# Another written order of the opening's steps and first loads in a fused attention and mixture kernel

## The chip, the cores and the metric

One core of one Trainium2 chip. The metric is the device time of one execution in microseconds. Five instruction streams matter: PE (TensorE, matmuls), DVE (VectorE), ACT (ScalarE), POOL (GpSimd) and SP (SyncE, which issues the input transfers).

## The reference, cut to what matters

```python
# q, k, v: 8 batches x 8 heads x 576 positions x 64, float32
scores = q @ k.T / 8
mask: heads 0-3 the last 32 positions, heads 4-7 every 32nd position before
attn = softmax(where(mask, scores, -1e9))        # max, exp, sum, divide
x = (attn @ v), heads side by side               # 4608 tokens x 512
h = maximum(maximum(x @ w1, x @ w2), x @ w3)     # 512 -> 768
out = h @ w_out                                  # 768 -> 512
```

## The kernel before, in words

The products `x @ w` are made in two parts: a float32 value is split into a high part (`xh`, `hh`) and a low part (`xl`, `hl`) that TensorE multiplies exactly enough, and the weights are split alike. Most of the program's later part (lines 789 and 887) works on sums of weights that the opening builds and writes to a scratch area in memory. The opening computes the first attention units, the first 512 tokens of the mixture directly (lines 522 and 552), and prepares the weights.

The order of the opening is written out by hand as a string of steps, `OPENING`; a loop executes it, and `pin` keeps each engine's instructions in that written order. A step is a letter and a number. One attention unit `n` (one batch, a pair of heads; units 0 to 3 belong to batch 0, 4 to 7 to batch 1, unit 8 to batch 2) passes through:

- `S n` scores on PE: for batch 0 first a mask matmul (L306), then L337, or L315 for the strided units from 4 on; `U n` (ACT L292) first copies the unit's keys into pairs for L315
- `X n` the masking and the maximum on DVE (L358, L366 and L367; for units in `APART` L358, L363 and L364)
- `E n` exponentials on ACT (L383, one instruction), or `G n` exponentials apart (L375, ten instructions with their sums, ten more records); units 2 and 7 are apart in both versions
- `N n` probabilities and the transpose on DVE (L394 to L397, L404)
- `V n` the product with v on PE (L481, L441 or L470), `H n` its high part (ACT L495), `L n` its low part (DVE L500)

A weight tile passes through `A` (ACT L164, POOL L165), `K` (ACT L170), `B` (DVE L180 and L183), `D` (POOL L193) and `C` (ACT cast L202, POOL L203). `F n` is 12 matmuls of line 522 into one result tile (two result tiles, used in turn), and `f`/`g` are the two halves of one of these: `f` needs units 1 and 0's columns (features 256 to 511), `g` those of units 2 and 3. `M n` reads the result out. `O n` is 18 matmuls of line 552, `Q n` its store, `T` prepares the second chunk of tokens, `W n` issues the writes of built weights to scratch from SP.

Scores have two places in TensorE's result memory. One serves units 0 and 2, the other, `s_ps` of pool `ps_s`, all the others, so `S8` may start only when the transpose of unit 7 (L404 in `N7`) has read it:

```python
s_ps = s_places[0 if n in (0, 2) else 1]
```

`LOADS` is the order in which SP issues the first input transfers: `q n` is the queries' piece and then the keys' piece of unit n, `v n` pieces of v, `w n` one weight tile each. SP is one queue, and a transfer whose buffer or semaphore isn't free holds up those behind it. From unit 4 on, `S n` also issues the q load of unit n+2.

Of the kernel before, what the change touches and what calls it, by code (L numbers as in the profile page):

```python
# [50 lines left out]
A12, A11, A22, S4, S2, S1, S3 = range(7)  # L51
# [1 line left out]


LOADS = """
q0 q0 w0 w1 q1 w2 q1 w3 v0 w4 w5 q2 q2 v0 v0 v0 w6 q3 q3 v1 v1 v1 v2 v2 v2 v1 v4 v2 w7 w8 v2 w9 v5 q4 q4 v3 v3 v3 v3
v3 w10 w11 v4 v4 w12 w13 q5 v4 v5 v5 v5 q5
"""
OPENING = """
S0 A0 X0 K0 A1 K1 K2 B0 D0 S1 B1 E0 N0 D1 A2 C0 S2 A3 B2 C1 A4 X1 B3 B4 K3 X2 D2 K4 E1 D3 N1 C2 C3 A5 A6 K5 V0 H0 L0  # L60
B5 B6 S3 D4 X3 D5 K6 D6 G2 C4 N2 C5 C6 E3 V1 H1 L1 V2 A7 A8 W0 N3 K7 A9 H2 f0 f1 U4 K8 K9 B7 S4 B8 D7 D8 C7 L2 V3 C8
H3 L3 A10 A11 W2 g0 B9 D9 M0 K10 K11 g1 F2 B10 D10 M1 C9 K12 X4 A12 C10 A13 F3 M2 F4 B11 K13 M3 F5 B12 E4 N4 U5 M4 D11
D12 C11 A14 C12 S5 M5 F6 F7 B13 B14 D13 K14 K15 K16 V4 K17 W3 X5 M6 M7 D14 F8 C13 A15 A16 C14 A17 B15 W1 D15 B16 D16
M8 E5 B17 N5 D17 K18 F9 M9 F10 A18 F11 C15 B18 M10 C16 K19 C17 A19 A20 K20 M11 S6 K21 X6 F12 B19 A21 D18 E6 W7 B20 D19
D20 W5 M12 F13 H4 F14 C18 K22 M13 F15 C19 C20 W4 A22 A23 K23 N6 B21 D21 V5 S7 M14 H5 B22 M15 B23 F16 F17 D22 D23 X7
C21 C22 C23 M16 M17 V6 T2 W8 O0 O1 G7 N7 H6 U8 T3 Q1 Q0 V7 S8 X8 O2 T0 Y0 Z0 U9 H7 E8 Q2 N8 Y1 O3 T1 Q3 W6
"""
APART = [int(step[1:]) for step in OPENING.split() if step[0] == "G"]

# [920 lines left out]
```

## Time and profile before

| | us |
|---|---|
| median of 3 runs | 668.78 (666.77 to 670.19) |
| the profiled execution | 667.13 |
| its span in the profile | 665.4 |
| PE busy in the span | 643.8 (97%) |
| DVE, ACT, POOL busy | 370.4, 337.3, 301.5 |

The profiled execution's time holds 1.7 us around its span. Numbers in square brackets in a row of the timeline are the idle time of the engine just before, with what ended it. Busy shares are means over stages with different limits: PE is busy without a break from 43.8 us on, and has its gaps ahead of that.

### The profile page before, as it was taken

What the parts mean: (1) busy time and instruction counts of PE and PEld (TensorE: products, weight loads), DVE (VectorE), ACT (ScalarE), POOL (GpSimd) and SP (SyncE); (2) the same over time, 40 slices, a digit from 0 to 9 for tenths busy, and PEclk for the clock granted to TensorE, in tenths of its full rate; (3) what the DMA queues carried; (4) which work ended last, traced back from release to release, by engine and by line L of the source; (5) the groups of instructions that cost most, each with busy time, mean ns of one, the idle gap of its engine ahead of it and who ended that gap; (6) DMA issues with size and microseconds to landing.
All of it is one profiled execution on the core that took longest, in us unless ns stands there. A gap on an engine that the chain in (4) does not pass through costs nothing.

```text
span 665.4 us, 18035 instructions
## 1 busy us (share of the span) xinstructions
PE 643.8 (97%) x7408; PEld 553.0 (83%) x7408; DVE 370.4 (56%) x515; ACT 337.3 (51%) x702; POOL 301.5 (45%) x291
## 2 busy tenths in 40 slices
PE   4599999999999999999999999999999999999997
PEld 3478888788778988988888888889999888999986
DVE  5878866576774647378355665743264662314340
ACT  4867666344364445546455456544444564444441
POOL 8979998799932423420233424004432402444410
PEclk9989999999999999999999999999999999999999
DMA  9799956747689777752487787336966614777411
GB/s 303 228 262 376 331 162 215 233 156 245 186 270 346 254 235 238 246 189 79 151 300 237 246 257 234 119 107 172 285 211 190 177 64 131 218 217 215 122 47 64
DMA packets 89370, 138.36 MB, mean 208 GB/s; under 512 B 10152, under 2 KB 39592, under 8 KB 89288
## 3 DMA queue, kind: packets, MB, share of 16 engines
q1 hardware_dynamic: 85256, 129.86, 62.1%
q10 hardware_dynamic: 4032, 7.34, 3.0%
q8 instruction: 59, 0.97, 0.6%
q14 instruction: 23, 0.19, 0.1%
HBM read 111.21 MB, written 25.95 MB: 206 GB/s over the span
## 4 chain that ended last, share of the span: by engine, by line
PE 81%; POOL 8%; DMA 1%; SPq 1%; ACT 1%; issue 1%; DVE 1%; POOLq 0%; DVEq 0%; ACTq 0%
PE f_ps L789 46%; PE f_ps L887 17%; PE f_ps L522 9%; PE f_ps L552 3%; POOL work L593 2%; PE o_ps L441 2%; PE o_ps L470 2%; PE s_ps L315 2%; POOL work L585 2%; POOL work L609 1%; PE s_ps L337 1%; POOL hl L543 1%; POOL sums_low L593 1%; POOL sums_low L585 1%; POOL sums_low L609 1%
## 5 line engine op out<-in xcount | busy, mean ns | idle before, releaser
L789 PE MATMUL f_ps<-xc,w_stream 128*128 128x448 f32 x1512 | 315.6, 368 | 0.6 <-DMA w_stream<-scratch 0.3
L789 PEld LDWEIGHTS f_ps<-xc,w_stream 128*128 128x128 f32 x1512 | 281.6, 188 | 27.4 <-ACT snap L840 2.3
L840 ACT COPY snap<-f_ps 128x448 f32<-128x448 f32 x240 | 128.0, 534 | 161.5 <-PE f_ps L789 160.7
L854 DVE TENSOR_TENSOR h_all<-h_all,snap 128x448 f32<-128x448 f32 x96 | 80.7, 881 | 145.5 <-POOL snap L852 145.4
L852 POOL TENSOR_TENSOR snap<-snap 128x448 f32<-128x448 f32 x72 | 89.8, 1253 | 143.7 <-ACT snap L840 103.1
L852 POOL TENSOR_TENSOR h_all<-snap 128x448 f32<-128x448 f32 x36 | 41.4, 1152 | 170.3 <-ACT snap L840 169.0
L887 PE MATMUL f_ps<-wNone,h_parts 128*128 128x512 f32 x504 | 115.1, 389 | 0.0
L887 PEld LDWEIGHTS f_ps<-wNone,h_parts 128*128 128x128 f32 x504 | 94.5, 188 | 19.8 <-ACT snap L840 0.2
L522 PE MATMUL f_ps<-xh,w 128*128 128x512 f32 x288 | 95.9, 402 | 0.0
L522 PEld LDWEIGHTS f_ps<-xh,w 128*128 128x128 f32 x288 | 54.8, 190 | 12.8 <-ACT xh L495 0.4
L522 PE MATMUL f_ps<-xl,w 128*128 128x512 f32 x144 | 56.9, 395 | 0.4 <-DVE xl L500 0.4
L878 DVE TENSOR_TENSOR h_parts<-h_all,h_parts 128x768 fp32r<-128x768 f32 (+2 forms) x40 | 27.2, 711 | 28.3 <-ACT h_parts L877 28.2
L893 ACT COPY work<-f_ps 128x512 f32<-128x512 f32 x28 | 16.4, 587 | 43.8 <-PE f_ps L887 43.8
L686 DVE TENSOR_TENSOR xc<-x_block,xc 128x896 fp32r<-128x896 f32 x28 | 29.8, 1087 | 11.7 <-ACT xc L683 6.9
L404 DVE STREAM_TRANSPOSE pt<-s_ps 128x640 f32<-128x640 f32 (+2 forms) x32 | 32.5, 1016 | 1.1
L522 PEld LDWEIGHTS f_ps<-xl,w 128*128 128x128 f32 x144 | 27.5, 191 | 6.0 <-DVE xl L500 0.7
L877 ACT CAST h_parts<-h_all 128x768 fp32r<-128x768 f32 (+2 forms) x40 | 24.5, 642 | 14.6 <-DVE h_all L854 7.7
L552 PE MATMUL f_ps<-wNone,hh 128*128 128x512 f32 x96 | 30.6, 400 | 0.0
L383 ACT ACTIVATE s_ps<-s_ps 128x640 f32<-128x640 f32 (+2 forms) x30 | 19.5, 649 | 20.3 <-DVE s_ps L367 20.3
L394 DVE TENSOR_REDUCE s_ps<-s_ps 128x10 f32<-128x640 f32 (+2 forms) x30 | 23.1, 771 | 10.8 <-ACT s_ps L383 10.8
L358 DVE TENSOR_TENSOR s_ps<-s_ps,mloc 128x640 f32<-128x640 f32 x14 | 11.6, 831 | 30.2 <-PE s_ps L337 30.1
L683 ACT CAST xc<-x_block 128x896 fp32r<-128x896 f32 x28 | 25.7, 943 | 5.4 <-DVE x_block L689 2.9
(87 smaller groups left out, 683.3 us busy)
## 6 DMA issues: line engine op xcount, KB each, us to landing
w_stream<-scratch SPq DMA_DIRECT2D x252, 256.0 KB, 3.9
w<-in_w SPq DMA_DIRECT2D x18, 512.0 KB, 7.6
qk_t<-in_qT SPq DMA_DIRECT2D x28, 288.0 KB, 4.3
qk_t<-in_kT SPq DMA_DIRECT2D x28, 288.0 KB, 5.9
v_t<-in_v_str SPq DMA_DIRECT2D x56, 128.0 KB, 3.9
out<-work ACTq DMA_DIRECT2D x28, 256.0 KB, 2.1
scratch<-w SPq DMA_DIRECT2D x27, 256.0 KB, 3.5
v_t<-in_v_loc SPq DMA_DIRECT2D x48, 96.0 KB, 3.0
```

Source lines behind the costliest of these rows:

```text
L404: pin(nc.vector.transpose(pt[:, :, : nm * at], s_ps[:, :, : nm * at]))
L522: pin(nc.tensor.matmul(f_ps, w[:, kc, :], x[:, kc, :], start=(kc == 2 and n == 0), stop=(kc == 1 and n == 2)))
L552: pin(nc.tensor.matmul(f_ps, h[:, ts], w, start=(j == 0 and n == 0), stop=(j == NJ - 1 and n == 2)))
L683: pin(nc.scalar.copy(out=x[m][:, 0], in_=src))
L686: pin(nc.vector.tensor_tensor(out=x[m][:, 1], in0=src, in1=x[m][:, 0].bitcast(F32), op=ALU.subtract))
L789: pin(nc.tensor.matmul(out_, w[:, wl, fs], x[:, xl, k, :], start=start and k == 0 and n == 0, stop=k == 1 and n == 2, skip_group_check=not ...
L840: pin(nc.scalar.copy(out=t, in_=src))
L852: pin(nc.gpsimd.tensor_tensor(out=h if i == 0 else u, in0=u, in1=t, op=ALU.add))
L854: pin(nc.vector.tensor_tensor(out=h, in0=h, in1=u, op=ALU.max))
L877: pin(nc.scalar.copy(out=to[:, 0, j0:j1], in_=src))
L878: pin(nc.vector.tensor_tensor(out=to[:, 1, j0:j1], in0=src, in1=to[:, 0, j0:j1].bitcast(F32), op=ALU.subtract))
L887: pin(nc.tensor.matmul(outs[t], h, w, start=(j == 0 and n == 0), stop=(j == NJ - 1 and n == 2)))
```

## The change

Two strings are replaced: the order of the first loads, and the order of the opening's steps. No instruction is added for the computation, and none is taken away. On SP the three scratch writes of the first `W` step stand amid the loads (ahead of the loads of v for unit 3) instead of behind all of them.

```diff
--- before.py
+++ after.py
@@ -53,17 +53,17 @@
 
 
 LOADS = """
-q0 q0 w0 w1 q1 w2 q1 w3 v0 w4 w5 q2 q2 v0 v0 v0 w6 q3 q3 v1 v1 v1 v2 v2 v2 v1 v4 v2 w7 w8 v2 w9 v5 q4 q4 v3 v3 v3 v3
-v3 w10 w11 v4 v4 w12 w13 q5 v4 v5 v5 v5 q5
+q0 q0 w0 w1 w2 q1 q1 w3 w4 q4 v0 v0 v0 v0 w5 w6 q2 q2 q3 q3 v1 v1 v1 v1 v2 q4 v2 v2 v2 w7 v2 w8 v5 v4 w9 v3 v3 v3 v3
+v3 v4 w10 w11 w12 w13 v4 v4 v5 v5 q5 q5 v5
 """
 OPENING = """
-S0 A0 X0 K0 A1 K1 K2 B0 D0 S1 B1 E0 N0 D1 A2 C0 S2 A3 B2 C1 A4 X1 B3 B4 K3 X2 D2 K4 E1 D3 N1 C2 C3 A5 A6 K5 V0 H0 L0
-B5 B6 S3 D4 X3 D5 K6 D6 G2 C4 N2 C5 C6 E3 V1 H1 L1 V2 A7 A8 W0 N3 K7 A9 H2 f0 f1 U4 K8 K9 B7 S4 B8 D7 D8 C7 L2 V3 C8
-H3 L3 A10 A11 W2 g0 B9 D9 M0 K10 K11 g1 F2 B10 D10 M1 C9 K12 X4 A12 C10 A13 F3 M2 F4 B11 K13 M3 F5 B12 E4 N4 U5 M4 D11
-D12 C11 A14 C12 S5 M5 F6 F7 B13 B14 D13 K14 K15 K16 V4 K17 W3 X5 M6 M7 D14 F8 C13 A15 A16 C14 A17 B15 W1 D15 B16 D16
-M8 E5 B17 N5 D17 K18 F9 M9 F10 A18 F11 C15 B18 M10 C16 K19 C17 A19 A20 K20 M11 S6 K21 X6 F12 B19 A21 D18 E6 W7 B20 D19
-D20 W5 M12 F13 H4 F14 C18 K22 M13 F15 C19 C20 W4 A22 A23 K23 N6 B21 D21 V5 S7 M14 H5 B22 M15 B23 F16 F17 D22 D23 X7
-C21 C22 C23 M16 M17 V6 T2 W8 O0 O1 G7 N7 H6 U8 T3 Q1 Q0 V7 S8 X8 O2 T0 Y0 Z0 U9 H7 E8 Q2 N8 Y1 O3 T1 Q3 W6
+A0 S0 A1 X0 E0 S1 A2 K0 K1 B0 B1 B2 N0 D0 C0 A3 B3 A4 B4 K2 V0 D1 D2 K3 K4 C1 C2 X1 S2 K5 E1 N1 A5 H0 L0 X2 B5 D3 D4
+A6 K6 S3 B6 V1 C3 C4 D5 G2 U4 X3 E3 H1 C5 N2 A7 A8 L1 V2 N3 D6 H2 B7 B8 K7 K8 f0 S4 f1 W2 D7 D8 C6 L2 A9 K9 X4 C7 C8
+V3 H3 L3 K10 B9 A10 B10 g0 M0 D9 A11 g1 E4 D10 M1 K11 C9 K12 A12 F2 F3 M2 M3 C10 A13 U5 K13 B11 B12 W1 K14 F4 F5 D11
+N4 S5 D12 C11 A14 M4 M5 X5 B13 K15 C12 D13 B14 D14 F6 M6 E5 C13 A15 C14 K16 K17 F7 A16 A17 M7 F8 N5 V4 M8 F9 M9 B15
+D15 A18 F10 B16 B17 D16 D17 C15 S6 C16 C17 K18 K19 F11 M10 F12 A19 A20 A21 B18 D18 X6 E6 M11 M12 B19 D19 F13 W3 K20
+K21 B20 H4 M13 K22 D20 F14 W5 F15 B21 C18 C19 D21 C20 K23 V5 A22 N6 A23 M14 M15 H5 W6 C21 S7 X7 G7 W4 B22 B23 F16 M16
+F17 U8 D22 D23 C22 V6 C23 W0 N7 M17 T3 H6 T0 S8 X8 T2 O0 O1 W7 Q0 V7 H7 T1 O2 Q1 O3 E8 N8 U9 Y1 Q2 Q3 W8 Y0 Z0
 """
 APART = [int(step[1:]) for step in OPENING.split() if step[0] == "G"]
```

PE, end of the opening, before: the last rows of `O1` (L552), `V7` (L441), `S8` (L315) and the first rows of `O2`. Just ahead of `O0` and `O1` stand `S7`, `F16`, `F17` and `V6`.

```order
L552 MATMUL f_ps_792<-wNone_1562,hh 128x512 x2
L552 MATMUL f_ps_792<-wNone_1562,hl 128x512
L441 MATMUL o_ps<-pt,v_t 64x64 x14
L441 MATMUL o_ps<-pt,v_t 64x32 x8
L441 MATMUL o_ps<-pt,v_t 64x64 x14
L441 MATMUL o_ps<-pt,v_t 64x32 x6
L315 MATMUL s_ps<-qk_t,pt 64x2x18 x32
L552 MATMUL f_ps_793<-wNone_1393,hh 128x512 x2
```

After: the last two rows of `V6`, then `S8`, and `O0`.

```order
L441 MATMUL o_ps<-pt,v_t 64x64 x14
L441 MATMUL o_ps<-pt,v_t 64x32 x6
L315 MATMUL s_ps<-qk_t,pt 64x2x18 x32
L552 MATMUL f_ps_794<-wNone_1403,hh 128x512 x2
L552 MATMUL f_ps_794<-wNone_1403,hl 128x512
L552 MATMUL f_ps_794<-wNone_1406,hh 128x512 x2
L552 MATMUL f_ps_794<-wNone_1406,hl 128x512
```

`S8` has moved ahead of `O0`, `O1` and `V7`: between `S7` and `S8` there are now only `F16`, `F17` and `V6`.

ACT, around the exponentials of unit 2 (`G2`, L375), before: the cast of a weight, the casts and copies of unit 0 (`H0`, L495), `K5` (L170), `G2`, then the casts of `C4`, `C5`, `C6` (L202), `E3` (L383) and `H1`.

```order
L170 ACTIVATE w_1_183<-w_1_183 128x512
L495 CAST xh<-o_ps 128x512
L495 COPY x_one<-o_ps 128x64
L170 ACTIVATE w_2_191<-w_2_191 128x512
L375 ACTIVATE s_ps,sm<-s_ps,mx 128x64 x10
L202 CAST w_1_641<-work 128x512
L202 CAST w_1_649<-work 128x512
L202 CAST w_2_652<-work 128x512
L383 ACTIVATE s_ps<-s_ps 128x2x320
L495 CAST xh<-o_ps 128x512
```

After: `H0`, `A6`, `K6`, then the casts of `C3` and `C4`, `G2`, the copies of `U4` (L292), `E3` and `H1`.

```order
L495 CAST xh<-o_ps 128x512
L495 COPY x_one<-o_ps 128x64
L164 ACTIVATE work<-w_2_190 128x512
L170 ACTIVATE w_2_190<-w_2_190 128x512
L202 CAST w_1_686<-work 128x512
L202 CAST w_1_689<-work 128x512
L375 ACTIVATE s_ps,sm<-s_ps,mx 128x64 x10
L292 COPY pt<-qk_t 128x2x8x18 x2
L292 COPY pt<-qk_t 128x2x8x14 x2
L383 ACTIVATE s_ps<-s_ps 128x2x320
L495 CAST xh<-o_ps 128x512
```

Two casts, each of which waits for POOL's addition (`D`), now stand ahead of `G2`, one (`C5`) stands behind `H1`, and `U4` has come forward to stand ahead of `E3`.

DVE, the low parts of units 2 and 3 (`L2`, `L3`, L500), before: the last row of `B8`, `L2`, `L3`, `B9`.

```order
L183 SCALAR_TENSOR_TENSOR work<-w_2_210,o_ps 128x512
L500 TENSOR_TENSOR xl<-o_ps,xh 128x480
L500 TENSOR_TENSOR xl<-o_ps,xh 128x32
L500 TENSOR_TENSOR xl<-o_ps,xh 128x480
L500 TENSOR_TENSOR xl<-o_ps,xh 128x32
L180 TENSOR_SCALAR o_ps<-work 128x2x256
```

After: the last row of `B8`, `L2`, the masking and maximum of unit 4 (`X4`), `L3`, `B9`.

```order
L183 SCALAR_TENSOR_TENSOR work<-w_2_212,o_ps 128x512
L500 TENSOR_TENSOR xl<-o_ps,xh 128x480
L500 TENSOR_TENSOR xl<-o_ps,xh 128x32
L358 TENSOR_TENSOR s_ps<-s_ps,mpair 128x32x18
L366 TENSOR_REDUCE mx<-s_ps 128x16
L367 TENSOR_TENSOR s_ps<-s_ps,mx 128x32x18
L500 TENSOR_TENSOR xl<-o_ps,xh 128x480
L500 TENSOR_TENSOR xl<-o_ps,xh 128x32
L180 TENSOR_SCALAR o_ps<-work 128x2x256
```

`X4`'s three rows stand between `L2` and `L3`; before they stood behind `M0`.

## Rows read from the trace of the kernel before

**Rows 1.** Busy time of the engines by stretches of the span. Columns: stretch and its length in us, then for PE, its weight loads, DVE, ACT and POOL the busy us and the instructions, the clock that TensorE was granted (1.00 is full), the busy share of the DMA engines and their GB/s.

```profile
10.00:20.00 10.00, 4.53 (x165) 3.14 (x165) 9.06 (x17) 5.94 (x11) 8.68 (x9) 1.00 1.08 310
...
31.50:38.30 6.80, 5.11 (x92) 4.33 (x93) 5.48 (x10) 3.96 (x10) 3.26 (x5) 0.50 0.95 265
...
43.80:60.00 16.20, 16.18 (x130) 13.28 (x131) 15.30 (x24) 12.49 (x24) 15.81 (x16) 1.00 1.08 336
60.00:200.00 140.00, 139.86 (x2070) 112.17 (x2069) 97.77 (x141) 74.13 (x170) 119.26 (x114) 1.00 0.72 233
```

**Rows 2.** All waits of PE in the first 140 us: line that waited, what it waited for, us in total, times, longest.

```profile
PE s_ps L337 <- DMA qk_t<-in_kT: 5.6, 2, 5.2
PE o_ps L441 <- DVE xl L500: 4.1, 2, 3.7
PE s_ps L306 <- POOL mstr L112: 2.8, 1, 2.8
PE s_ps L306 <- DVE pt L404: 2.1, 2, 1.3
PE s_ps L337 <- DMA v_t<-in_v_str: 2.1, 1, 2.1
PE f_ps L522 <- DVE xl L500: 0.4, 1, 0.4
```

**Rows 3.** The chain of work that ended last in the first 140 us, its part around units 7 and 8, in order of time: start us, us, engine and line. L337 is `S7`, L522 `F16` and `F17`, the first L441 `V6`, L552 `O0` and `O1`, the second L441 `V7`, L315 `S8`.

```profile
88.80 0.90 PE s_ps L337 x61
89.70 5.71 PE f_ps L522 x24
95.41 1.07 PE o_ps L441 x66
96.48 8.59 PE f_ps L552 x36
105.07 1.07 PE o_ps L441 x68
106.14 1.07 PE s_ps L315 x64
```

**Rows 4.** Timeline of DVE, then of ACT, from 88 to 113 us: start us, us, engine, line, operation. DVE: first and last row of `X7`, first and last row of `N7`, first and last row of `X8` (128x576). ACT: first and last of the 20 rows of `G7` (L375), and `U8`'s copies or those of `U9`, the same operation.

```profile
92.51 0.82 DVE L358 TENSOR_TENSOR s_ps<-s_ps,mloc 128x640 f32<-128x640 f32 x1
...
94.24 0.17 DVE L364 TENSOR_SCALAR mx<-s_ps 128x10 f32<-128x10 f32 x1
...
101.59 0.42 DVE L395 TENSOR_SCALAR sm<-sm 128x10 f32<-128x10 f32 x1 [3.25 <-ACT s_ps L375]
...
103.16 0.85 DVE L404 STREAM_TRANSPOSE pt<-s_ps 128x640 f32<-128x640 f32 x1
...
107.28 0.77 DVE L358 TENSOR_TENSOR s_ps<-s_ps,mpair 128x576 f32<-128x576 f32 x1 [2.31 <-PE s_ps L315]
...
108.87 0.77 DVE L367 TENSOR_TENSOR s_ps<-s_ps,mx 128x576 f32<-128x576 f32 x1
...
97.21 0.28 ACT L375 ACTIVATE s_ps<-s_ps,mx 128x64 f32<-128x64 f32 x1
...
101.36 0.19 ACT L375 ACTIVATION_READ_ACCUMULATOR s_ps<-s_ps,mx 128x1 f32 x1
...
102.13 1.38 ACT L292 COPY pt<-qk_t 128x288 f32<-128x288 f32 x4
```

**Rows 5.** Timeline from 15 to 46 us, the way to `G2`, in the order POOL, ACT, PE: POOL's additions and subtractions of two weight tiles; ACT's first and last row of `G2`, and the load wait ahead of `A9`; PE's `S2`.

```profile
18.10 2.54 POOL L193 TENSOR_TENSOR work<-work,w 128x512 int32<-128x512 int32 x2
20.59 2.52 POOL L203 TENSOR_TENSOR w<-work,w 128x512 fp32r<-128x512 f32 x2
23.07 1.20 POOL L165 TENSOR_SCALAR work<-work 128x512 f32<-128x512 f32 x2
...
24.17 0.29 ACT L375 ACTIVATE s_ps<-s_ps,mx 128x64 f32<-128x64 f32 x1
...
28.32 0.19 ACT L375 ACTIVATION_READ_ACCUMULATOR s_ps<-s_ps,mx 128x1 f32 x1
...
35.38 0.68 ACT L164 ACTIVATE work<-w 128x512 f32<-128x512 f32 x1 [2.00 <-DMA w<-in_w]
...
19.60 1.35 PE L337 MATMUL s_ps<-qk_t 64*32 64x64 f32 x72 [2.11 <-DMA v_t<-in_v_str]
```

**Rows 6.** Timeline from 15 to 46 us, the way from `G2` to `g0`, DVE, then PE. DVE: first row of `N2`, last row of `N3`, first row of `B7`, `L2`, `L3`. PE: `V2`, `V3`, and the first row of L522 that reads `L3`'s result (`g0`).

```profile
29.65 0.91 DVE L395 TENSOR_SCALAR sm<-sm 128x10 f32<-128x10 f32 x1
...
35.25 0.85 DVE L404 STREAM_TRANSPOSE pt<-s_ps 128x640 f32<-128x640 f32 x1
37.21 0.69 DVE L180 TENSOR_SCALAR o_ps<-work 128x512 int32<-128x512 int32 x1 [1.11 <-POOL work L165]
...
40.07 0.75 DVE L500 TENSOR_TENSOR xl<-o_ps,xh 128x480 fp32r<-128x480 f32 x2
43.01 0.76 DVE L500 TENSOR_TENSOR xl<-o_ps,xh 128x480 fp32r<-128x480 f32 x2 [2.19 <-ACT x_one L495]
...
33.19 1.66 PE L441 MATMUL o_ps<-pt,v_t 32*64 32x64 f32 x84 [3.72 <-DVE xl L500]
...
40.87 1.14 PE L441 MATMUL o_ps<-pt,v_t 32*64 32x64 f32 x84 [0.37 <-DVE xl L500]
...
43.82 0.50 PE L522 MATMUL f_ps<-xl,w 128*128 128x512 f32 x1 [0.40 <-DVE xl L500]
```

## Prediction

> **What bounds the kernel now.** I read the stretches first. From 43.8 us on PE is the bound without a gap: 16.18 us busy of 16.20, then 139.86 of 140 [rows 1]. So the end can move in two ways only: PE reaches that dense part at another time, or a new wait opens in it. The waits of PE come next: in the first 140 us they sum to 17.1 us, each with a named releaser, and the last of them is the 0.4 us of `g0` at 43.82 for `L3` [rows 2, 6]. Between `S7` and `S8` the chain of waits is PE alone, row upon row: `S7` ends at 89.70, `S8` starts at 106.14 [rows 3]. No wait is left unexplained, so nothing here shows a price of fetching instructions that another layout could win back.
>
> The sum is made against the profiled execution (667.13, of which 665.4 span); the median is 668.78, and I add the differences to that.
>
> **The change part by part.** First `S8`. It needs the place in which unit 7's scores stand, so it waits for the last row of `N7`. From the end of `S7` the way there is `X7`, 94.24 + 0.17 - 92.51 = 1.90; `G7`, 101.36 + 0.19 - 97.21 = 4.34; `N7`, 103.16 + 0.85 - 101.59 = 2.42 [rows 4]. That is 8.66, and with four hand-offs of about 0.05 (`L3` ends at 43.77 and PE starts at 43.82 [rows 6]) 8.85 us. Before, PE had 16.44 us of work between (106.14 - 89.70), and the transpose ended at 104.01, so `S8` waited for nothing. After, only `F16`, `F17` and `V6` stand between: 5.71 + 1.07 = 6.78 [rows 3]. PE then stands still for 8.85 - 6.78 = 2.1 us. Its queue is in order, so `O0`, `O1` and `V7`, 8.59 + 1.07 us of work that may be ready, stand behind `S8` and can't fill the gap. The bounds: 1.9 with no hand-offs at all; and 104.01 - 89.70 - 6.78 = 7.5 if `X7` and `G7` came as late as before. They came late there for written order: `X7` began 2.8 us after `S7` and `G7` 2.8 us after `X7`, behind other steps of DVE and ACT. After, `X7` stands ahead of `B22` and `B23`, and `G7` behind one cast only, so I take 2.2, near the lower end. `U8`, which `S8` needs too, stands behind `G7` on ACT with 1.38 us [rows 4], less than `N7`'s 2.42, and costs nothing; without that cover it would be 1.38.
>
> Does a gap of 2.2 us cost more than itself? In this trace the clock was 0.50, the lower of its levels, in 31.5 to 38.3 [rows 1], in which PE stood still for 3.72 us until 33.19 [rows 6]. The wait of 2.1 us ahead of 19.60 lies in a stretch granted 1.00 [rows 1, 5]. A wait of 2.2 is nearer to the second, so I add nothing; the other end is half of a stretch like the first, 6.8 / 2 = 3.4 us. The Trainium skill, "TensorE: Matmul & The Clock Gate", section "HAM oscillation — how this bites in real kernels", says that gaps without matmuls let the gate drop back to half rate, and each next burst then starts slow; by that rule the gap would cost up to the 3.4 more, while the row of the shorter wait doesn't show it.
>
> Second, the way to `g0`. Before, `G2` runs from 24.17 to 28.51 [rows 5], `N2` starts at 29.65, and DVE is then filled by `N2`, `L1`, `N3` until 36.10, 6.45 us [rows 6]. After, `G2` stands behind the casts of `C3` and `C4`. The addition that `C4` needs is the end of this row on POOL, counted from the end of `A4`: `D1` `D2` 2.54, `C1` `C2` 2.52, half of 1.20 for `A5`, `D3` `D4` 2.54 [rows 5], 8.2 together. `A4`'s part on POOL ended at about 18.1 before; after, fewer steps stand ahead of it, and I put it at 17.0 to 18.1. So the addition ends at 25.2 to 26.3, the cast (0.62) lies behind it, and `G2` starts at 25.9 to 26.9 instead of 24.17. Its data is also later: the keys of unit 2 now lie behind 1.04 MB more of loads (by `LOADS` and the tiles' shapes a weight tile of 512 x 256 values, 0.52 MB, a piece of unit 4's q, 0.29, and three pieces of v for unit 0, 0.22), at 310 GB/s [rows 1] 3.4 us; `S2` at 19.60 becomes 23.0, and with 1.35 and `X2`'s 1.0 that gives `G2` at 25.3 at the earliest, which is less than the casts' wait. I take 26.1: `G2` ends at 30.45 and `N2` starts there, 0.8 later than before.
>
> From there DVE's queue: `N2` to `N3` 6.45, to 36.9; `B7` `B8` 2.94 (37.21 to 40.15 before), to 39.9, without the 1.11 of waiting that stood there [rows 6]; `L2` 0.75; now `X4`, taken as `X8` of the same form, 108.87 + 0.77 - 107.28 = 2.36 [rows 4]; `L3` 0.76. That ends at 43.8, the same as before (43.77): `X4` goes into the 2.19 us in which DVE waited ahead of `L3`. The other way into `L3` is PE's: `V2` waits for `L1` and starts 0.8 to 0.9 later (33.19 before), `f0`, `S4` and `f1` follow unchanged, `V3` loses its wait of 0.37, so it ends about 0.5 later; then `H3`, `L3`, `g0`. That gives +0.5. With more hand-offs in a queue that now has no idle time, I take +0.7; the bounds are -0.9 (43.77 - 1.11 - 2.19 + 2.36 = 42.83, if `G2` weren't later at all) and +1.6 (`G2` at 26.9).
>
> Third, the rest. `F`, `M`, `O` and `Q` keep their numbers and lengths, and the orders of `A` to `D` between 44 and 88 us change beside a dense PE: DVE is busy 97.77 and ACT 74.13 of 140 us [rows 1], so their cover is the PE work itself; if it failed, each late cast would cost its 0.62 and one addition, 1.3. On SP the three writes of `W1` stand ahead of v for unit 3 and `w9`, and wait for `C4`'s subtraction, about 2.5 us behind its cast, 28.5 to 29. Loads queue behind them. Before, `w9` was the load that ACT awaited until 35.38 [rows 5], ahead of `H2`. After, `A9` stands behind `H2` and ahead of `H3`, which is due at about 42.3: 6.9 us later. The cost is nothing below a delay of 6 us or so; above, it goes to `g0` one for one. I take 0.
>
> Sum: 2.2 + 0.7 = 2.9 us. The profiled execution would come to 670.0, the median to 671.7.
>
> **The rivals.** *The clock falls in `S8`'s wait*: for it the 0.50 behind the wait of 3.72, against it the shorter waits at 1.00. Up to 3.4 us more, since all behind is dense: 675.1. *A late load*: `w9` or v for unit 3 behind the scratch writes hold `H3` or `V3`, or the q load of unit 6 comes late; loads run at 265 GB/s there [rows 1] and have 6 us of slack, so one more 0.5 MB tile (2 us) wouldn't show, three would: +1 to +2.5, about 673.5. *`S8` is covered*, the change does nothing there: `F16` or `F17` themselves come late, waiting for a weight, so that the gap lies ahead of them or isn't there; only the front counts, 669.5. *The other side*: `g0` comes earlier. DVE loses two waits of 3.3 us together and takes up 2.36, so with `G2` on time `g0` lies 0.9 earlier, and with `S8` covered the time is 667.9. To be faster by over 0.5% (3.3 us, about what a measurement of this kernel can tell from no change) `g0` would have to be reached before 40.5; with `N2` not ahead of 29.65 and 10.1 us of DVE work up to the end of `L2` alone, then `V3`, `H3` and `L3` in turn, that is out by these rows. The two ends differ by the point where `G2` starts: before 24.2 it gains, behind 25.3 it loses.
>
> **How the numbers follow.** The sum as it stands has a chance of 0.57, 670.0 to 673.2 by its bounds; the clock 0.12; a late load 0.12; `S8` covered 0.13; the other side 0.06. The likeliest gives 671.7. 669.2 to 675.0 leaves out most of the other side, a part of the covered case and of the clock's. The line of +0.5% lies at 672.1, inside the likeliest case: somewhat over half of it is below, with the covered and the other case 0.49 within; slower 0.48 (the rest of the likeliest, the clock, most of the late loads); faster 0.03.
>
> **What would show it.** The profile after should have a wait of PE at line 315 for line 404 of about 2.2 us near 97 us, and a dense PE on both sides of it; granted clock 1.00 in the 10 us behind it; the first L375 of `G2` at about 26; `X4` between `L2` and `L3` with no idle time ahead of `L3`; `g0`'s start at 44.5. The prediction is wrong if `G7` stands behind a waiting cast (the wait at line 315 is then 4 or more), if the clock shows 0.50 near 97 us, or if PE waits for a load between 36 and 44 us.

## The result, and the profile after

The changed kernel took 673.68 us in the median of 6 runs (671.47 to 674.28) beside 668.68 of before (666.77 to 671.29): a ratio of 1.0058, 95% interval 1.0031 to 1.0084 (the two medians alone give 1.0075, inside it). Its profiled execution took 674.28 us, span 672.5, so 7.15 us more than that of before. TensorE's busy time by stretches, columns as in [rows 1]:

```profile
31.40:38.30 6.90, 2.18 (x153) 1.89 (x148) 5.71 (x11) 5.16 (x16) 3.27 (x5) 0.70 0.89 279
38.40:43.80 5.40, 4.54 (x71) 3.44 (x74) 3.58 (x6) 3.64 (x8) 2.01 (x2) 0.50 0.75 192
43.80:60.00 16.20, 15.79 (x177) 12.61 (x172) 13.01 (x23) 11.19 (x25) 14.87 (x16) 0.98 1.06 295
60.00:200.00 140.00, 137.60 (x2117) 110.25 (x2116) 95.70 (x139) 73.38 (x170) 125.20 (x119) 1.00 0.69 224
```

Between 60 and 200 us PE is now idle for 2.4 us (0.14 before), and the half clock reaches to 43.8 and, by the 0.98 of the next stretch, about 0.6 us beyond. Its waits in the first 140 us, to be read against [rows 2]:

```profile
PE s_ps L337 <- DMA qk_t<-in_kT: 6.5, 2, 6.1
PE o_ps L481 <- DVE work L183: 6.2, 1, 6.2
PE o_ps L441 <- DVE xl L500: 3.3, 1, 3.3
PE s_ps L306 <- POOL mstr L112: 2.9, 1, 2.9
PE o_ps L441 <- issue: 2.4, 1, 2.4
PE s_ps L315 <- ACT wNone L202: 2.3, 1, 2.3
PE o_ps L481 <- ACT s_ps L375: 1.6, 1, 1.6
PE f_ps L522 <- DVE xl L500: 0.4, 1, 0.4
```

In sum the waits are 25.6 us (17.1 before). Four things are new: `S8` (line 315) waits 2.3 us; `V0` (line 481) waits 6.2 us for a step of DVE on the place that it shares with the weights; `V1` (line 481) waits 1.6 us, and `B6` on that same place ends at 30.80, 0.1 us ahead of it, although the row names ACT; and `V2` (line 441) stands still for 2.4 us with no releaser ("issue").

The wait of `S8`, DVE then PE: `X7` from its first to its last row, `N7` likewise, and `S8`; to be read against [rows 4].

```profile
94.84 0.83 DVE L358 TENSOR_TENSOR s_ps<-s_ps,mloc 128x640 f32<-128x640 f32 x1 [1.79 <-PE s_ps L337]
...
96.58 0.17 DVE L364 TENSOR_SCALAR mx<-s_ps 128x10 f32<-128x10 f32 x1
...
101.22 0.44 DVE L395 TENSOR_SCALAR sm<-sm 128x10 f32<-128x10 f32 x1 [1.03 <-ACT s_ps L375]
...
102.89 0.85 DVE L404 STREAM_TRANSPOSE pt<-s_ps 128x640 f32<-128x640 f32 x1
...
103.84 1.14 PE L315 MATMUL s_ps<-qk_t,pt 64*64 64x36 f32 x64 [2.26 <-ACT wNone L202]
```

`N7`'s transpose ends at 102.89 + 0.85 = 103.74 and `S8` starts at 103.84, so DVE ends the wait; the row names a cast of ACT that ended earlier.

The way to `g0`, ACT (`A4`'s weight tile, first row of `G2`), DVE (last row of `N3`), PE (`V0`, `S2`, `V2` in two pieces, `g0`); against [rows 5, 6]:

```profile
18.13 0.66 ACT L164 ACTIVATE work<-w 128x512 f32<-128x512 f32 x1 [1.83 <-DMA w<-in_w]
...
28.10 0.28 ACT L375 ACTIVATE s_ps<-s_ps,mx 128x64 f32<-128x64 f32 x1
...
40.03 0.85 DVE L404 STREAM_TRANSPOSE pt<-s_ps 128x640 f32<-128x640 f32 x1 [2.36 <-PE o_ps L441]
...
21.05 2.11 PE L481 MATMUL o_ps<-pt,v_t 18*64 18x18 f32 x128 [6.16 <-DVE work L183]
...
25.52 1.36 PE L337 MATMUL s_ps<-qk_t 64*32 64x64 f32 x72
...
35.66 1.25 PE L441 MATMUL o_ps<-pt,v_t 32*64 32x64 f32 x59 [3.33 <-DVE xl L500]
39.26 0.67 PE L441 MATMUL o_ps<-pt,v_t 32*64 32x64 f32 x25 [2.35 <-issue]
...
48.92 0.50 PE L522 MATMUL f_ps<-xl,w 128*128 128x512 f32 x1 [0.41 <-DVE xl L500]
```

`g0` starts 48.92 - 43.82 = 5.10 us later than before. Of this, 2.47 is `V2`'s later start (35.66 for 33.19) and 2.35 the stall inside it; from `V2` the way goes through PE's rows to `V3` and `g0`, since DVE had 1.09 us of idle time left ahead of `L3`. With the 2.26 of `S8` that is 7.4, and the span is longer by 7.1: the rest of the program adds nothing.

### The profile page after: what moved, and what is told of

It is laid out like the page before. It is cut to its first block, busy times and chain, and to the rows that moved or that the text cites. A ratio compares the mean times of both kernels' runs of the same rounds, so it can differ in the third digit from the quotient of the medians.

```text
span 672.5 us, 18034 instructions
## 1 busy us (share of the span) xinstructions
PE 642.9 (96%) x7408; PEld 552.8 (82%) x7408; DVE 372.0 (55%) x515; ACT 337.4 (50%) x702; POOL 301.3 (45%) x291
## 4 chain that ended last, share of the span: by engine, by line
PE 90%; ACT 3%; DMA 2%; SPq 2%; DVE 1%; issue 1%; POOL 0%; ACTq 0%
PE f_ps L789 46%; PE f_ps L887 17%; PE f_ps L522 14%; PE f_ps L552 4%; PE o_ps L441 2%; PE s_ps L315 2%; PE o_ps L470 2%; PE s_ps L337 2%; DMA qk_t<-in_qT 2%; ACT s_ps L375 1%; SPq L243 1%; SPq L152 0%; POOL work L193 0%; SPq L277 0%; ACT pt L292 0%
## 5 line engine op out<-in xcount | busy, mean ns | idle before, releaser
L522 PE MATMUL f_ps<-xh,w 128*128 128x512 f32 x288 | 95.8, 402 | 0.0
L522 PEld LDWEIGHTS f_ps<-xh,w 128*128 128x128 f32 x288 | 54.6, 189 | 12.5 <-ACT xh L495 0.3
L522 PE MATMUL f_ps<-xl,w 128*128 128x512 f32 x144 | 56.8, 394 | 0.4 <-DVE xl L500 0.4
L893 ACT COPY work<-f_ps 128x512 f32<-128x512 f32 x28 | 16.4, 587 | 43.8 <-PE f_ps L887 43.6
L522 PEld LDWEIGHTS f_ps<-xl,w 128*128 128x128 f32 x144 | 27.3, 190 | 5.8 <-DVE xl L500 0.7
L552 PE MATMUL f_ps<-wNone,hh 128*128 128x512 f32 x96 | 30.6, 400 | 0.0
L383 ACT ACTIVATE s_ps<-s_ps 128x640 f32<-128x640 f32 (+2 forms) x30 | 19.6, 652 | 19.2 <-DVE s_ps L367 19.2
L358 DVE TENSOR_TENSOR s_ps<-s_ps,mloc 128x640 f32<-128x640 f32 x14 | 11.6, 831 | 31.7 <-PE s_ps L337 31.5
```

What stands on the lines that cost most here:

```text
L522: pin(nc.tensor.matmul(f_ps, w[:, kc, :], x[:, kc, :], start=(kc == 2 and n == 0), stop=(kc == 1 and n == 2)))
L552: pin(nc.tensor.matmul(f_ps, h[:, ts], w, start=(j == 0 and n == 0), stop=(j == NJ - 1 and n == 2)))
```

## The experiments

Each kernel is the changed one, or the one before, with the edit shown. Ratios are to runs of the kernel before on the same chip in the same session.

**The changed kernel once more**, for what differs from execution to execution.

> The changed kernel unaltered, for a second look. Theory 'race' (the stalls without a releaser are late instruction fetches: each block of 127 matmuls is asked for when TensorE passes the edge before, comes 5 to 8 us later, and the edges lie at the 476th, 603rd and 731st matmul): the profile either shows a stall at V1's 59th or V2's 59th matmul, or none; if none, g0 starts at 45.5 to 47.2 and this execution takes 2 to 3 us less than the first profile (674.3), if there is one, at 48 to 50. Rival (the stall belongs to the written order and is there each time): the same stall of 2.0 to 2.7 us at V2's 59th, g0 at 48.5 to 49.5.

673.04 us in the median (670.43 to 676.63, 10 runs), ratio 1.0057 (1.0024 to 1.0090). ACT (`A4`, `G2`), PE (`V2` in two pieces, `g0`), DVE (first row of `N7`), PE (`S8`), and the stretch behind `S8`'s wait:

```profile
15.93 0.66 ACT L164 ACTIVATE work<-w 128x512 f32<-128x512 f32 x1 [1.65 <-DMA w<-in_w]
...
25.90 0.28 ACT L375 ACTIVATE s_ps<-s_ps,mx 128x64 f32<-128x64 f32 x1
...
33.45 1.25 PE L441 MATMUL o_ps<-pt,v_t 32*64 32x64 f32 x59 [3.28 <-DVE xl L500]
35.03 0.67 PE L441 MATMUL o_ps<-pt,v_t 32*64 32x64 f32 x25 [0.33 <-issue]
...
44.80 0.50 PE L522 MATMUL f_ps<-xl,w 128*128 128x512 f32 x1 [0.40 <-DVE xl L500]
...
97.12 1.52 DVE L395 TENSOR_SCALAR sm<-sm 128x10 f32<-128x10 f32 x1 [0.52 <-ACT s_ps L375]
...
100.82 1.94 PE L315 MATMUL s_ps<-qk_t,pt 64*64 64x36 f32 x64 [3.34 <-issue]
...
100.80:104.60 3.80, 3.78 (x69) 3.38 (x70) 2.60 (x3) 2.89 (x8) 3.17 (x3) 0.55 1.00 314
```

The same program reaches `g0` at 44.80 here and at 48.92 in the first profile. Two things differ. `A4` found its weight tile at 15.93 instead of 18.13, and `G2` follows it by the same distance in both: 25.90 - 15.93 = 9.97 and 28.10 - 18.13 = 9.97 (a third execution of these steps, below, has 29.32 - 19.36 = 9.96). And the stall in `V2` is 0.33 instead of 2.35 us. The expectation put `g0` at 48 or later if there is a stall; a short one was not thought of. The rival, a stall of the same length each time, is out. `S8` waited 3.34 here, and behind it the clock was granted 0.55 over 3.8 us. The 1.08 us more than in the first profile are those of `N7`'s first row, 1.52 us for 0.44; its transpose ends at 100.72, 0.1 us ahead of `S8`, so this "issue" is a wait for DVE and not a stall like that of `V2`. Why the row took longer isn't shown.

**S8 moved back** behind `V7`.

```diff
-... T3 H6 T0 S8 X8 T2 O0 O1 W7 Q0 V7 H7 ...
+... T3 H6 T0 T2 O0 O1 W7 Q0 V7 S8 X8 H7 ...
```

> The changed kernel with S8 and X8 written behind V7 again, as in the kernel before; nothing else is moved. My theory (the wait of S8 for the last row of N7 costs its whole length, since all behind it is dense): the wait of 2.3 us at line 315 is gone, no other wait takes its place between 90 and 125 us, and the time falls by 2.2 to 2.4 us to about 671.3. Rival (the wait only stands where another one of O0 would have stood, for hl or the last weights): a wait of 1 us or more appears at line 552 and the time falls by less than 1.2.

671.70 us (670.63 to 673.15, 6 runs), ratio 1.0046 (1.0029 to 1.0062). ACT (`A4`, `G2`), PE (`V2`, `g0`, the first wait of `O0`'s), and POOL (the low part of the last block, `M17`):

```profile
19.36 0.66 ACT L164 ACTIVATE work<-w 128x512 f32<-128x512 f32 x1 [1.26 <-DMA w<-in_w]
...
29.32 0.28 ACT L375 ACTIVATE s_ps<-s_ps,mx 128x64 f32<-128x64 f32 x1
...
36.87 1.65 PE L441 MATMUL o_ps<-pt,v_t 32*64 32x64 f32 x84 [3.39 <-DVE xl L500]
...
47.13 0.50 PE L522 MATMUL f_ps<-xl,w 128*128 128x512 f32 x1 [0.41 <-DVE xl L500]
...
105.55 0.50 PE L552 MATMUL f_ps<-wNone,hl 128*128 128x512 f32 x1 [1.22 <-POOL hl L543]
...
103.73 1.77 POOL L543 TENSOR_TENSOR hl<-h_max,hh 128x512 fp32r<-128x512 f32 x1
```

The wait at line 315 is gone, and `O0` waits 1.22 us at line 552 for `hl`, which POOL finishes at 105.50. So of 2.25 us of waiting about 1.0 is given back: the rival was right on this. In the ratio it is 0.1% (0.8 us) beside the changed kernel's 1.0057 and 1.0058, by the medians' distance from the kernel before 1.7 to 2.2 us; the intervals can't tell. The spans behind `g0`'s start tell more, since the front drops out of them: 621.6 us in the kernel before, 622.8 in both kernels with `S8` back (this one and the last of those with other loads, below), 623.6 and 624.2 in the two with `S8` forward whose clock stayed behind a wait of 2.2 us (the first profile and the 64 matmuls, below), and 624.8 to 625.4 in four whose clock fell. Beside `S8` back, its place costs 0.8 to 1.4 us where the clock stays, and 2.0 to 2.6 where it falls. `V2` ran in one piece here, with the same front.

**S8 ahead of O0 in the kernel before**, a larger dose of the same wait.

```diff
-... V6 T2 W8 O0 O1 G7 N7 H6 U8 T3 Q1 Q0 V7 S8 X8 O2 ...
+... V6 T2 W8 G7 N7 U8 S8 O0 O1 H6 T3 Q1 Q0 V7 X8 O2 ...
```

> The kernel before with S8 alone moved ahead of O0 on TensorE (and the copies of U8 ahead of those of H6 on ACT); X7, G7 and N7 stay where they are on DVE and ACT. Theory (the price of S8 is what its chain needs from S7's end less the work that stands between): the chain ends at 104.0 in the kernel before and V6 at 96.5, so TensorE waits 7.5 us at line 315 and the time rises by 7.3 to 7.7 to 676.3. Rival (most of the wait is caught by other waits that O0 or the later steps would have had, as line 552's 1.2 us when S8 was moved back): a rise of less than 6.3.

677.74 us (677.12 to 679.30, 4 runs) beside 670.25, ratio 1.0105 (1.0062 to 1.0147), 7.0 us by it and 7.5 by the medians. PE (`V1` from its 60th matmul, `S8`), and the stretch behind:

```profile
32.46 1.26 PE L481 MATMUL o_ps<-pt,v_t 18*64 18x18 f32 x69 [3.10 <-issue]
...
105.64 1.94 PE L315 MATMUL s_ps<-qk_t,pt 64*64 64x36 f32 x64 [7.54 <-ACT xh L227]
...
105.60:109.00 3.40, 3.36 (x68) 3.04 (x69) 2.16 (x3) 0.01 (x1) 1.38 (x2) 0.51 0.10 21
```

The wait came to 7.54 for 7.5 expected (`N7`'s transpose ends at 105.54, 0.1 us ahead of `S8`; the row names ACT). Behind `g0` this execution is 8.4 us longer than the kernel before, so nothing of note caught the wait. Behind it the clock was granted 0.51 for 3.4 us. Ahead of it this execution has a stall of 3.10 us without a releaser in `V1`, in steps and loads that are the kernel before's own: that kernel isn't free of such stalls either, its profiled execution was.

**Loads alone, steps alone**: the kernel before with the changed `LOADS`, and the changed kernel with the `LOADS` of before.

```diff
-q0 q0 w0 w1 q1 w2 q1 w3 v0 w4 w5 q2 q2 v0 v0 v0 w6 q3 q3 v1 v1 v1 v2 ...      (LOADS; OPENING of before kept)
+q0 q0 w0 w1 w2 q1 q1 w3 w4 q4 v0 v0 v0 v0 w5 w6 q2 q2 q3 q3 v1 v1 v1 v1 v2 ...
```

> The steps of the kernel before with the loads of the changed kernel. In the changed kernel the weight tiles of A3 and A4 are awaited until 15.6 and 18.1 us (13.9 and no wait before), and g0 starts 5.1 us later than before. Theory 'loads' (the order of the loads brings w3 and w4 later, and from there the way to g0): A3 starts at 15 or later here too, and g0 at 46 to 47.5; time 671 to 672. Theory 'steps' (the written order of V0, S2 and the casts ahead of G2 does it): g0 within 1 us of 43.8, time 668 to 669.7.

The other one is the same difference the other way round, in the changed kernel.

> The steps of the changed kernel with the loads of the kernel before. Theory 'loads': A3 and A4 come at 14 and 15.8 as before, g0 at 45 to 46.5, time 670.5 to 672. Theory 'steps': G2 starts behind 27.5 all the same, g0 at 47.5 to 49, time 672.5 to 674. The wait of S8 stays at 2.3 us in both.

Loads alone: 674.73 us (674.42 to 675.01), ratio 1.0091 (1.0074 to 1.0108). Steps alone: 680.61 us (679.93 to 681.66), ratio 1.0181 (1.0161 to 1.0200). PE (`S2`, and `V1` from its 60th matmul) and ACT (`A9`) of the first:

```profile
23.48 1.35 PE L337 MATMUL s_ps<-qk_t 64*32 64x64 f32 x72 [6.76 <-DMA qk_t<-in_kT]
...
33.99 1.26 PE L481 MATMUL o_ps<-pt,v_t 18*64 18x18 f32 x69 [1.09 <-issue]
...
42.16 0.69 ACT L164 ACTIVATE work<-w 128x512 f32<-128x512 f32 x1 [4.47 <-DMA w<-in_w]
```

ACT (`U4`) and PE (`V2`) of the second:

```profile
39.60 1.45 ACT L292 COPY pt<-qk_t 128x288 f32<-128x288 f32 x4 [6.41 <-DMA qk_t<-in_qT]
...
43.05 1.65 PE L441 MATMUL o_ps<-pt,v_t 32*64 32x64 f32 x84 [9.93 <-DVE xl L500]
```

Each half alone costs more than both together. With the new loads `S2` waits for its keys until 23.48 (19.60 before [rows 5]), and `A9` for its tile until 42.16 (35.38 before [rows 5]), which in the old steps stands ahead of `H2`; the new steps have it behind. With the old ones `U4`, which now stands ahead of `E3` and `H1`, waits 6.4 us for unit 4's q, and `V2` for 9.9. The loads had to be changed for `U4`'s place, and the price is unit 2's keys and `w9`. The two theories both fell: neither string alone explains the 5.1 us.

**S2 ahead of V0**, and then also the casts of `C3` and `C4` behind `U4`.

```diff
-... K2 V0 D1 D2 K3 K4 C1 C2 X1 S2 K5 ...
+... K2 D1 D2 K3 K4 C1 C2 X1 S2 V0 K5 ...
```

> The changed kernel with V0 behind S2 on TensorE, as in the kernel before. In the changed kernel S2 stands behind V0, which waits until 21.05 for the last step on the shared place o_ps (B4, and so A4's weight tile); X2 ends at 28.0 and C4's cast, also ahead of G2, at 28.2. Theory 'tie': S2 comes at 23.2 to 23.6, with the keys, X2 ends at 25.5 to 26, but G2 still waits for C4 and starts behind 27.5; the time falls by less than 1. Rival 'S2 alone': G2 starts with X2 near 26 and the time falls by 2 or more.

```diff
-... S3 B6 V1 C3 C4 D5 G2 U4 X3 ...
+... S3 B6 V1 D5 G2 U4 C3 C4 X3 ...
```

> As e6, and the casts of C3 and C4 behind G2 and U4, so that both things that hold G2 are undone. Theory 'tie': G2 starts at 25.5 to 26.5 and N2 at 30 to 31, g0 comes 1.5 to 2.5 us earlier than in the changed kernel's profile without its fetch stall (47.1 in e1), at 44.8 to 45.8; time 670.5 to 672. Rival (the casts ahead of G2 cost nothing, since weights follow them anyway): as e6.

674.63 us (672.76 to 678.25), ratio 1.0052 (1.0026 to 1.0078), and 676.29 us (675.35 to 677.71), ratio 1.0088 (1.0053 to 1.0123). ACT of the first (`G2`), then of the second (`G2`):

```profile
30.64 0.29 ACT L375 ACTIVATE s_ps<-s_ps,mx 128x64 f32<-128x64 f32 x1
```

```profile
28.94 0.29 ACT L375 ACTIVATE s_ps<-s_ps,mx 128x64 f32<-128x64 f32 x1 [0.57 <-DVE mx L364]
```

Nothing was gained, and the second expectation (`G2` at 25.5 to 26.5) was wrong by 2.4 us; a stall of 3.27 us ahead of `V1`'s 60th matmul comes on top in the second. With `V0` behind `S2`, `V0` waits for the keys of unit 2, `H0` on ACT and `L0` on DVE wait for `V0`, and `X2` stands behind `L0`. With `V0` first `G2` hangs on `w4`, with `S2` first on the keys of unit 2: on a late load either way.

**Two more weights and unit 2's q earlier** in the loads; then the same with `S8` back.

```diff
-q0 q0 w0 w1 w2 q1 q1 w3 w4 q4 v0 v0 v0 v0 w5 w6 q2 q2 ...
+q0 q0 w0 w1 w2 w3 w4 q1 q1 q2 q2 v0 v0 v0 v0 w5 q4 w6 ...
```

> The steps of the changed kernel, with w3, w4 and the two pieces of unit 2's q ahead in the loads, and the first piece of unit 4's q later (between w5 and w6). Theory 'loads' (w4 at 18.1 and the keys of unit 2 at 23.2 hold G2): A4 starts before 16.5, S2 before 22, G2 at 25 to 26.5, and g0 1.5 to 3 us earlier than in the changed kernel with the same fetch stalls (45.9 without one in the first profile, 47.1 in e1); time 671 to 672.5. Rival 'steps' (the order of the casts and of V0 holds it anyway): G2 behind 27.5, time 673 to 674.5.

> The loads of e10, and S8 with X8 behind V7. If both prices are separate and add up, 0.8 to 2 us below e10 (line 552 waits 1.2 us for hl instead of line 315's 2.2), 669.5 to 671; if the front's gain only moves the waits at 97 us, as e10.

672.91 us (671.65 to 675.90), ratio 1.0051 (1.0022 to 1.0080), and 671.89 us (669.93 to 675.60), ratio 1.0035 (1.0005 to 1.0066). PE (`V0` from its 86th matmul) and ACT (`G2`) of the first, and the stretch from the end of `V2` to `H3`:

```profile
21.85 0.88 PE L481 MATMUL o_ps<-pt,v_t 18*64 18x18 f32 x43 [1.29 <-issue]
...
27.47 0.29 ACT L375 ACTIVATE s_ps<-s_ps,mx 128x64 f32<-128x64 f32 x1 [1.69 <-DVE mx L364]
...
37.40:46.40 9.00, 9.00 (x161) 6.81 (x161) 6.57 (x10) 4.79 (x10) 7.38 (x7) 0.51 1.05 281
```

`A4` starts at 14.99, but `S2` stands behind a stall of 1.29 us in `V0`, and `G2` starts at 27.47, later than the theory of the loads had it and at the edge of its rival. Then the half clock stayed for 9.0 us, and `g0` came at 48.09. `S8` back gave 1.0 us of the medians; 671.89 is 0.9 above the expectation for it.

**Matmuls added ahead of V2**, to move it along the instruction stream.

```diff
+        if n == 1:
+            for _ in range(64):
+                pin(nc.tensor.matmul(s_ps[:, 0, :1], unit, mstr[:, :1], start=True, stop=True))
```

> The changed kernel with 64 more matmuls of one column (a TensorE instruction pair each, about 0.05 us) ahead of S1's mask, in the 6 us in which TensorE waits for unit 1's keys; their result is overwritten. In the changed kernel TensorE stands still for 2.35 us in the middle of V2, at its 59th of 84 matmuls, with no releaser, while an instruction fetch is under way. Theory 'fetch' (the stall stands at a place of the instruction stream): it moves 64 matmuls forward, ahead of V2's first matmul, where TensorE waits for L1 anyway until 35.7, and g0 comes 1.2 to 2.4 us earlier; time 671.5 to 672.7. Rival (something that belongs to V2 itself, or the load of the transfers at that time): the stall stays at V2's 59th matmul, time as the changed kernel.

```diff
+            for _ in range(32):
+                pin(nc.tensor.matmul(s_ps[:18, 0, :18], unit[:18, :18], mstr[:18], start=True, stop=True))
```

> The dose of e4 with cheap matmuls: 32 of 18x18 (two TensorE passes each, 64 in the trace, about 0.7 us together) in the wait of S1; their result is overwritten. The stalls without a releaser stood at the 731st matmul of the stream in the changed kernel, the 603rd in e2, the 477th in e4: steps of 127. Theory 'block': with 64 more ahead of V2 the 731st is the fifth-last of V1 or so, ahead of a wait for L1 of 3 us; V2 runs its 84 matmuls in one piece and no stall shows between V2 and f0; time 671 to 672.5. Rival: V2 stalls at its 59th again, or the stall is now ahead of V1's end and L1 comes later by as much; time as the changed kernel, 673 to 674.5.

689.31 us, ratio 1.0313 (1.0292 to 1.0333): the 64 took 27.5 us for some 3 expected, as 128 in the trace, and filled far more than the wait, so its time says nothing. The 32 cheap ones took 2.3 us, inside the wait of `S1`: 680.26 us (679.23 to 684.21), ratio 1.0145 (1.0098 to 1.0193). The stall of each, in `V0` from its 86th and in `V1` from its 125th matmul:

```profile
38.69 0.88 PE L484 MATMUL o_ps<-pt,v_t 18*64 18x18 f32 x43 [1.09 <-issue]
```

```profile
37.54 0.40 PE L484 MATMUL o_ps<-pt,v_t 18*64 18x18 f32 x4 [3.67 <-issue]
```

In both the stall left `V2`'s 59th matmul and stood where the same count of matmuls from the start falls. But the gain expected of the second didn't come: the stall was 3.67 us long at the end of `V1`, so `H1` and `L1` came later by it. That was the rival's second half. It isn't all of the time: the added matmuls moved the later edges too, and behind `g0` this execution (684.21, the slowest of its four) has four more stalls without a releaser, at lines 340 and 318 (337 and 315 of the changed kernel), 0.4 to 1.4 us each and 3.4 together; no other kernel has one there.

**The stalls without a releaser, together.** Counted from the first matmul (64 passes of the pads and all), those of the first 60 us stand behind 349, 476, 603 or 731 matmuls (one more in two cases), steps of 127 or 128, in nine of the twelve programs. With its weight load a matmul is two instructions, and the page counts 59 transfers of instructions on queue q8 with 0.97 MB, 16.4 KB each; for 7,408 of each kind that is 126 pairs per transfer, so q8 is taken for TensorE's. The DMA queues of the changed kernel's first profile from 31.4 to 36.7 us, and q8 from 36.7 to 38.0:

```profile
q1 hardware_dynamic: 1440, 1.48, 86.0%
q14 instruction: 1, 0.01, 0.4%
```

```profile
q8 instruction: 1, 0.02, 4.8%
```

PE passed the edge at 603 matmuls at 31.45, and until 36.7 nothing was moved on q8, while the loads took 86% of the engines; the transfer came then, and PE went on at 39.26. In other executions it came about 3 us behind the edge (28.55 and 31.5 in the kernel before, where PE was waiting for `L1` and lost nothing). So a block seems to be asked for when TensorE enters the one ahead of it, and a burst of short matmuls runs into the next edge first: `V1`'s 128 last 1.43 us. That the stalls are waits for instructions is argued from their places and from these transfers; no row names it. The lag isn't one number either: in the same profile the two transfers ahead of this one started 1.0 us behind the matmul at its edge (349) and 0.4 us ahead of it (476). What makes a transfer start at once here and 5 us late there was not tried; the loads beside it are the nearest suspect.

## Why the prediction was right, and where its steps were off

The time lies inside the range and the direction is as forecast; 671.7 was 1.3 to 2 us too low. The range held by its width more than by the sum: the profiled execution came 7.15 us behind that of before, for 2.9 forecast, and what filled the rest was priced in the rivals or not at all. Its "670.0 to 673.2 by its bounds" isn't the sum of the bounds given, which reach from 669.8 to 677.9; it takes the wait of `S8` to 2.8 and no further. For the clock, two of the stretches behind a wait of 2.2 us at `S8`, in the first profile and in the kernel with `S2` ahead of `V0`:

```profile
103.80:107.00 3.20, 3.16 (x73) 2.79 (x74) 1.99 (x2) 2.65 (x8) 3.20 (x4) 1.00 0.92 312
```

```profile
106.00:109.00 3.00, 3.00 (x69) 2.57 (x70) 1.79 (x2) 2.51 (x8) 3.00 (x4) 0.67 0.99 331
```

And `A4` on ACT in the kernel before, which waited for POOL and not for its tile:

```profile
15.75 0.68 ACT L164 ACTIVATE work<-w 128x512 f32<-128x512 f32 x1 [0.62 <-POOL w L203]
```

- *`S8`'s wait, 2.2 us*: right. 2.26 in the profile, 2.21 to 2.24 in six of the variants, 3.34 once; and 7.54 for 7.5 in the kernel before. The chain is the sum that was made: `X7` 1.91 and `N7` 2.52 in the first profile, for 1.90 and 2.42, with `G7` as forecast between. The one longer wait came from one row of `N7`, 1.1 us longer than elsewhere.
- *`O0`, `O1` and `V7` "may be ready"*: only in part. `hl` is late as well, 1.22 us, so the wait by itself cost about 1.0 us net, and 2.0 to 2.6 with the clock.
- *No cost of the clock*: wrong in most executions. In the 3 to 3.8 us behind a wait of 2.2 it was granted 1.00 in two kernels (the first profile and the 64 matmuls), 0.57 to 0.72 in five; behind 3.34 it was 0.55, behind 7.5 0.51. At 0.67 over 3 us that is 1 us. Choosing by the one wait of [rows 5] without a fall was too narrow. The rival's 3.4 was too large. The Trainium skill, "TensorE: Matmul & The Clock Gate", section "HAM oscillation — how this bites in real kernels", says that waits without matmuls put the gate back, in a kernel whose waits are longer, 3 to 5 us; here 2.2 us was enough in five kernels of seven.
- *`g0` 0.7 later*: the mis-sized term. In the second execution it was 1.0 with `G2` at 25.90 (26.1 forecast); in the first 5.1, in the one with `S8` back 3.3. The step that failed is "`A4`'s part on POOL ... at 17.0 to 18.1": it took over a row of before in which `w4` was not awaited. With the new loads ACT waits for it until 15.9, 18.1 and 19.4 in three executions, and `G2` follows 10 us behind. The sum behind that step was right: `A4`'s part on POOL ended at 17.30 in the second execution and at 19.48 in the first, and the addition that `C4` needs 8.1 us behind the latter, for 8.2 forecast. The two kernels with `w4` earlier didn't win the time back: in them unit 1's keys came later instead, and a stall stood in `V0`. `S2`, put at 23.0 by its keys (they came at 23.48 with the loads alone), started at 25.52, because it stands behind `V0`, and `V0` behind `B4` and so behind the same tile; this wait was overlooked.
- *No price of instruction fetch*: wrong, if the stalls without a releaser are that. "No wait is left unexplained" held for one execution of the kernel before. In the changed kernel the stall in `V2` took 2.35 us, all of it on the way over PE to `V3` and `g0`; it also held up the transpose of `N3` (line 404) by 2.36, which DVE's idle time ahead of `L3` could partly take up.
- *The scratch writes amid the loads, `w9`, `X4` between `L2` and `L3`*: as forecast, no PE wait came of them in the profile; `X4` filled the idle time that DVE had ahead of `L3` down to 1.09 us, not to nothing.
- *The rivals*: the covered `S8` and the faster front are out; a late load came, but `w4`, not `w9` or v.

What stays open: how the median's 4.6 to 5.0 us divide. In the first profile they are 5.1 + 2.3, in the second 1.0 + 3.3 and what is left of 5.7, 1.4, about what the clock's 0.55 over 3.8 us costs (1.7); the executions scatter by 6 us, the kernel before's by 9 in its largest session, and no one profile stands for them.

## What to carry to other kernels

A step that needs the place of another one's result costs that one's whole chain less the work that stands between, and this could be summed from rows to a tenth in eight of nine executions; check also what the step behind it waits for, since that is the part that undoing doesn't give back. Before a load order is changed, list for each early step whether its load was awaited at all: a tile with no wait in the old profile has an unknown slack, not an endless one. Take two or three profiles where the front hangs on transfers, since one shows one draw.

## What the runs showed of the hardware that was not expected

TensorE stalled for 0.2 to 3.7 us at fixed counts of its instruction stream, 127 or 128 matmuls apart. The reading that fits is that a burst of short matmuls came to the edge before the next 16 KB of instructions: PE went on 1.2 to 1.6 us after a transfer had landed (37.8 and 39.26 in the first profile). The same 2.2 us of idle time was followed by full clock in two kernels and in five by 0.57 to 0.72 of it over 3 to 3.5 us.
